# A fused sliding-window attention and gated feed-forward kernel: an attention burst one gap later, another batch's bursts re-placed, and two more transposes given to the DMA crossbar

## The chip, the cores and the metric

The kernel runs on one core of a Trainium2 chip. The metric is the device time of one execution in microseconds; the time of a kernel is the median of several executions. Beside these times there is one execution recorded by the hardware profiler, with its trace. All positions below are microseconds from the start of that recording.

## The reference

Eight batches of eight heads attend over 576 positions with head size 64. A query sees the keys within 32 positions, eight global positions see everything, and everything sees them. The attention output is the input of a gated feed-forward block over 4608 tokens.

```python
    scores = scale * np.matmul(q, k.transpose(0, 1, 3, 2))
    mask = np.abs(pos[:, None] - pos[None, :]) <= window
    mask = mask | is_global[:, None] | is_global[None, :]
    scores = np.where(mask, scores, -1000000000.0)
...
    attn = np.exp(scores)
    attn = attn / (np.sum(attn, axis=-1, keepdims=True) + 1e-09)
    return np.matmul(attn, v).astype(np.float32)
...
    x = np.ascontiguousarray(attn_out.transpose(0, 2, 1, 3)).reshape(B * S, H * D)
    g = x @ w_gate
    silu = g * (1.0 / (1.0 + np.exp(-g)))
    val = x @ w_val
    return (silu * val @ w_out).astype(np.float32)
```

## The kernel before

The feed-forward block is the backbone. Its 4608 tokens are cut into nine chunks of 512, and each chunk is 16 *units* on TensorE: twelve `gate` units (lines 782 to 798), each eight matmuls of 512 columns into two banks of PSUM, and four `outp` units (lines 845 to 857) of twelve such matmuls each. After every unit comes a *gap*, into which the program puts small pieces of attention work. Gaps are numbered through, 16 to a chunk; the loop at lines 926 to 933 emits unit n and then the pieces of gap n. The order on each engine is the order in which the program emits: nothing is reordered later, so an instruction that waits holds up everything behind it on its engine.

Attention of batch b is spread over the gaps of the chunk before the one that needs it. `attention(b)` (line 348) returns a table from a relative gap number to a list of steps. The table of batch 1 is shifted by 3 (line 908) and that of batch b from 2 on by 16(b-1) (line 910). So relative gap 7 of batch 1 is gap 10, and relative gap 2 of batch 2 is gap 18. The steps of one batch:

- `step_GT` (line 399) transposes the gathered global keys and queries on TensorE; VectorE copies them out as `gT`.
- `step_S2` (line 438): scores of all keys against the global columns. It reads `kT`. ScalarE takes the exponential (`p2e`), VectorE masks it into `p2` (line 454).
- `step_SG` (line 416): scores of the global rows. It reads `qTs[b]`, that is `qT`. Result: `pg`.
- `step_P2T` (line 460): transposes `p2` into `p2t`. Below batch `XP` it does so by five transposes on TensorE and a copy on ScalarE; from batch `XP` on by one crossbar transpose, a DMA that SyncE issues (line 463).
- `step_AV2` (line 473): value products of the global rows from `p2t` and `va`; VectorE makes `gv` of them (lines 484 to 492).
- `step_S(u)`, u from 0 to 4 (line 497): local scores, 16 small matmuls (8 for u = 4), an exponential on ScalarE and a multiplication by the band on VectorE.
- `step_AV(tp)`, tp from 0 to 3, and `step_AV8` (lines 574 and 606): value products of 128 tokens each from the local probabilities, `pg` and `gv`. They read `va` and `vb`, a copy of `va` shifted by 64 rows. VectorE then normalises (lines 562 to 568). The PSUM pool "m" has one buffer, which most value products share, so a product waits until the one before it is normalised.
- `step_X` (line 630), `step_X01`, `step_X8`: transposition of the result into `xT`, the input of the gate units. From batch 2 on this is a crossbar transpose issued by SyncE.

From batch 2 on k and q arrive in three stages. GpSimd issues DMAs that cast k and q to bf16 in DRAM (`cast_qk`, line 106); SyncE issues crossbar transposes from there into `kT` and `qT` (`transpose_qk`, line 114, the issues at lines 116 and 120); TensorE reads these. `load_v` (line 97) has GpSimd load `va` in five blocks, and `load_vb` (line 124) has SyncE copy `va` to `vb` in two DMAs (lines 129 and 130).

SyncE's instructions are one queue in program order: `kT` and `qT` of batch b, results `out` (line 857), `vb`, `p2t` where it is a DMA, and the transposes of `xT`. For batch 2 the queue around the change reads: `kT`, `qT` of batch 2; four results; two `vb` of batch 2; `kT`, `qT` of batch 3; then the transposes of the results of batch 2.

Of the kernel before, what the change touches and what calls it, by code (L numbers as in the profile page):

```python
# [26 lines left out]
def kernel(  # L27
# [25 lines left out]
    KC = S + 2 * WIN  # L53
    XQ = 2
    XB = 2
    XP = 4
    W = D + 2

    assert (B, H, S, D, NG, DM, DF) == (8, 8, 576, 64, 8, 512, 1536)
# [288 lines left out]
    def attention(b):  # L348
# [111 lines left out]
        def step_P2T():  # L460
            if b >= XP:
                st["p2t"] = work.tile([P, 5, P], BF16, tag="p2t", name="p2t")
                nc.sync.dma_start_transpose(out=st["p2t"], in_=st["p2"])
                return
            ps = mtile([P, 5, P], BF16, "ps_p2t")
            for u in range(5):
                nc.tensor.transpose(
                    out=ps[:, u, :], in_=st["p2"][:, P * u : P * (u + 1)], identity=ident
                )
            st["p2t"] = work.tile([P, 5, P], BF16, tag="p2t", name="p2t")  # L470
            nc.scalar.copy(out=st["p2t"], in_=ps)
# [231 lines left out]
        L = lambda f, *a: (lambda: f(*a))  # L703
# [30 lines left out]
        if b == 1:  # L734
            return r | {
                5: [L(step_P2T), L(step_S, 0)],
                6: [L(step_S, 1), L(step_AV2)],
                7: [L(step_S, 2), L(step_AV, 0)],
                8: [L(step_S, 3), L(step_AV, 1)],
                9: [L(step_AV, 2)],  # L740
                10: [L(step_AV, 3), L(step_X01, 0)],
                11: [L(step_S, 4), L(step_X01, 1)],
                12: [L(step_AV8)], 13: [L(step_X8)],
            }
# [10 lines left out]
        if b == 2:  # L755
            return {
                1: [L(step_GT), vb],
                3: [L(step_S2), L(step_SG)],
                4: [L(step_S, 0), L(step_P2T)],
                6: [L(step_S, 1), L(step_AV2)],  # L760
                8: [L(step_S, 2), L(step_AV, 0), L(step_X, 0)],
                10: [L(step_S, 3), L(step_AV, 1), L(step_X, 1)],
                11: [L(step_S, 4), L(step_AV, 2), L(step_X, 2)],
                12: [L(step_AV, 3), L(step_AV8), L(step_X, 3), L(step_X8)],
            }
        return {
            1: [L(step_GT), vb],
            2: [L(step_S2), L(step_SG)] + ([L(step_P2T)] if b >= XP else []),
            4: [L(step_S, 0)] + ([] if b >= XP else [L(step_P2T)]),
            7: [L(step_S, 1), L(step_AV2)],  # L770
# [90 lines left out]


    head, xa1, xa2, xa3, s4, av8, x8 = attention(0)
    for f in head:
        f()
# [41 lines left out]
    for i, g in attention(1).items():  # L907
        gaps[3 + i] = gaps.get(3 + i, []) + g
    for b in range(XQ, B):
        o = 16 * (b - 1)  # L910
        for i, g in attention(b).items():
            gaps[o + i] = gaps.get(o + i, []) + g
        if b > 3:
            tr_at[b] = o - 16 + 5
        if b > 4:
            cast_at[b] = o - 32 + 8
        if b > 2:
            v_at[b] = o - 16 + 2
            if b % 2 == 0:
                g_at[b] = o - 16 + 6  # L920
                m_at[b] = o - 16 + 13
# [43 lines left out]
```

## Time and profile before

| | us |
|---|---|
| median of 5 runs | 358.0 (357.56 to 358.96) |
| the profiled execution | 357.52 |
| its span in the trace | 355.7 |
| TensorE busy | 344.5 (97%) |
| VectorE busy | 232.1 (65%) |
| ScalarE busy | 151.8 (43%) |
| GpSimd busy | 92.6 (26%) |

The granted TensorE clock is 1.00 over the whole span. The profiled execution is 0.48 us below the median of the runs, and 1.8 us of it lie outside the span. By stage, from the view of busy time in given stretches (busy time of TensorE and VectorE, mean busy share of the core's DMA engines):

| stretch, us | what runs there | TensorE | VectorE | DMA |
|---|---|---|---|---|
| 40.0 to 66.5 | rest of chunk 0, batch 1's attention | 25.82 of 26.50 | 15.14 | saturated, 182 GB/s |
| 66.5 to 93.0 | gates of chunk 1, batch 2's attention | 25.85 of 26.50 | 22.44 | saturated, 181 GB/s |
| 104.6 to 142.0 | chunk 2, batch 3's attention | 37.03 of 37.40 | 25.72 | saturated, 173 GB/s |
| 142.0 to 179.0 | chunk 3, batch 4's attention | 36.74 of 37.00 | 25.52 | 144 GB/s |

A gate unit takes TensorE about 1.73 us, an output unit about 2.6 us. A DMA in the trace has the time of its issue on its engine's queue, and a landing time, which is when its completion reached the semaphore that a reader waits for.

### The profile page before, as it was taken

What the parts mean: (1) busy time and instruction counts of PE and PEld (TensorE: products, weight loads), DVE (VectorE), ACT (ScalarE), POOL (GpSimd) and SP (SyncE); (2) the same over time, 40 slices, a digit from 0 to 9 for tenths busy, and PEclk for the clock granted to TensorE, in tenths of its full rate; (3) what the DMA queues carried; (4) which work ended last, traced back from release to release, by engine and by line L of the source; (5) the groups of instructions that cost most, each with busy time, mean ns of one, the idle gap of its engine ahead of it and who ended that gap; (6) DMA issues with size and microseconds to landing.
All of it is one profiled execution on the core that took longest, in us unless ns stands there. A gap on an engine that the chain in (4) does not pass through costs nothing.

```text
span 355.7 us, 7680 instructions
## 1 busy us (share of the span) xinstructions
PE 344.5 (97%) x3112; PEld 167.8 (47%) x3161; DVE 232.1 (65%) x470; ACT 151.8 (43%) x235; POOL 92.6 (26%) x110
## 2 busy tenths in 40 slices
PE   6989999999999999999999999999999999999996
PEld 2575545444444454444444444444444444444444
DVE  5868784389818873789368935894488637815850
ACT  4865662465325541554244523543254323323322
POOL 8984663905323314301290111000000000000000
PEclk9999999999999999999999999999999999999999
DMA  7999999999999999995899979813320230011002
GB/s 108 150 197 204 184 212 160 146 251 142 158 172 233 145 156 163 173 183 82 147 166 152 141 120 168 113 42 92 105 70 2 61 100 28 0 59 62 0 20 100
DMA packets 153540, 44.15 MB, mean 124 GB/s; under 512 B 140064, under 2 KB 148000, under 8 KB 153504
## 3 DMA queue, kind: packets, MB, share of 16 engines
q0 software_dynamic: 101216, 19.14, 68.3%
q1 hardware_dynamic: 52288, 24.51, 34.0%
q8 instruction: 25, 0.41, 0.5%
q14 instruction: 11, 0.09, 0.1%
HBM read 38.02 MB, written 16.52 MB: 153 GB/s over the span
## 4 chain that ended last, share of the span: by engine, by line
PE 84%; DMA 9%; POOL 4%; issue 1%; DVE 1%; ACT 0%; POOLq 0%
PE po L850 25%; PE pg L793 24%; PE pv L793 23%; DMA va<-in_v_dram 4%; DMA k_bf<-in_k_dram 3%; PE ps_av L595 3%; PE ps_s L508 3%; DMA vb<-va 2%; PE ps_av L586 1%; PE po L837 1%; POOL va L102 1%; PE ps_av L477 1%; PE ps_s L442 1%; PE ps_av L622 0%; PE ps_av L614 0%
## 5 line engine op out<-in xcount | busy, mean ns | idle before, releaser
L793 PE MATMUL pg<-xT,wg_sb 128*128 128x512 bf16 x399 | 107.0, 380 | 1.6
L793 PE MATMUL pv<-xT,wv_sb 128*128 128x512 bf16 x413 | 106.6, 379 | 0.1
L822 DVE SCALAR_TENSOR_TENSOR gv<-th,pg 128x512 bf16<-128x512 bf16 x107 | 73.3, 685 | 50.2 <-ACT th L820 49.3
L820 ACT ACTIVATE th<-pg 128x512 bf16<-128x512 f32 x107 | 63.9, 598 | 81.4 <-PE pg L793 79.5
L850 PE MATMUL po<-wo_sb,h 128*128 128x512 bf16 x400 | 92.4, 379 | 0.9 <-issue 0.2
L826 DVE TENSOR_TENSOR h<-gv,pv 128x512 bf16<-128x512 bf16 x107 | 73.5, 687 | 11.5 <-PE pg L793 0.5
L793 PEld LDWEIGHTS <-wv_sb 128*128 128x128 bf16 x424 | 41.5, 98 | 50.0
L850 PEld LDWEIGHTS <-h 128*128 128x128 bf16 x420 | 39.5, 98 | 45.4
L793 PEld LDWEIGHTS <-wg_sb 128*128 128x128 bf16 x424 | 38.4, 98 | 43.5 <-issue 1.7
L102 POOL DMA_DIRECT2D va<-in_v_dram x40 | 35.5, 993 | 82.7 <-PE ps_av L595 72.4
L855 ACT ACTIVATE osb<-po 128x512 f32<-128x512 f32 x35 | 20.9, 597 | 81.9 <-PE po L850 60.8
L541 ACT ACTIVATE pe<-ps_s 128x1024 bf16<-128x1024 f32 (+1 forms) x39 | 36.4, 936 | 17.0 <-PE ps_s L508 17.0
L547 DVE TENSOR_TENSOR pt<-pe,band 128x1024 bf16<-128x1024 bf16 (+1 forms) x39 | 24.7, 634 | 14.0 <-ACT pe L541 13.9
L568 DVE TENSOR_TENSOR xa<-ps_av,den 128x512 bf16<-128x512 f32 (+1 forms) x40 | 25.5, 638 | 1.4
L562 DVE TENSOR_REDUCE den<-ps_av 128x8 f32<-128x16 f32 (+1 forms) x40 | 6.7, 166 | 27.6 <-PE ps_av L595 25.2
L508 PEld LDWEIGHTS <-kT 64*128 64x128 bf16 x576 | 10.7, 95 | 15.5 <-issue 15.1
L109 POOL DMA_DIRECT2D kf<-in_k_dram x6 | 13.4, 2233 | 16.5 <-issue 10.2
L109 POOL DMA_DIRECT2D qf<-in_q_dram x6 | 15.4, 2564 | 3.9 <-DMA va<-in_v_dram 2.4
L508 PE MATMUL ps_s<-qT,kT 64*128 64x64 bf16 x576 | 15.3, 191 | 0.1
L595 PE MATMUL ps_av<-vb,pt 128*64 128x66 bf16 x256 | 14.2, 197 | 0.5 <-DMA vb<-va 0.5
L595 PE MATMUL ps_av<-va,pt 128*64 128x66 bf16 x256 | 14.4, 197 | 0.0
L595 PEld LDWEIGHTS <-pt 128*64 128x64 bf16 x512 | 10.8, 110 | 4.7 <-DMA vb<-va 0.6
(142 smaller groups left out, 198.3 us busy)
## 6 DMA issues: line engine op xcount, KB each, us to landing
out_dram<-osb SPq DMA_DIRECT2D x35, 256.0 KB, 2.6
vb<-va SPq DMA_DIRECT2D x14, 264.0 KB, 5.3
kf<-in_k_dram POOLq DMA_DIRECT2D x6, 576.0 KB, 18.3
qf<-in_q_dram POOLq DMA_DIRECT2D x6, 576.0 KB, 18.4
va<-in_v_dram POOLq DMA_DIRECT2D x24, 128.0 KB, 10.8
va<-in_v_dram POOLq DMA_DIRECT2D x16, 96.0 KB, 9.1
wg_sb<-in_moe_w_gate_dram POOLq DMA_DIRECT2D x3, 512.0 KB, 11.7
wv_sb<-in_moe_w_val_dram POOLq DMA_DIRECT2D x3, 512.0 KB
```

The costliest lines, as they stand in the source:

```text
L102: nc.gpsimd.dma_start(out=va[lo:hi, u, :, 0:D], in_=vs[t0 + lo : t0 + hi])
L109: nc.gpsimd.dma_start(out=t, in_=src[b].rearrange("h s d -> s h d"))
L508: nc.tensor.matmul(out=ps[:, par, 64 * slot : 64 * slot + 64], lhsT=kT[r : r + 64, hp, 64 * t : 64 * t + P], rhs=qTs[b][r : r + 64, hp, 64 ...
L541: nc.scalar.activation(out=pe, in_=ps[:, :, 0 : 64 * ns].rearrange("p r (s c) -> p r s c", c=64), func=AF.Exp, scale=SCALE,)
L547: mult = lambda: nc.vector.tensor_tensor(out=pt.rearrange("p r s c -> p (r s) c"), in0=pe.rearrange("p r s c -> p (r s) c"), in1=bc(band, ...
L568: nc.vector.tensor_tensor(out=xa.rearrange("p (g h) d -> p g h d", g=g), in0=bc(ps, pst + [[1, D]]), in1=bc(den, [[4, g], [1, 4], [0, D]]) ...
L595: nc.tensor.matmul(out=ps[64 * e : 64 * e + 64, hg, hl, :], lhsT=pt[:, hl % 2, 4 * (hl // 2) + 2 * (tp % 2) + e, :], rhs=(va if e == 0 els ...
L793: nc.tensor.matmul(out=ps[:, 0:n], lhsT=w[:, cc, P * fc : P * (fc + 1)], rhs=xT[:, cc, t0 : t0 + n], start=(cc == 0), stop=(cc == NCC - 1),)
L820: nc.scalar.activation(out=th[:, 0:n], in_=pg[:, 0:n], func=AF.Tanh, scale=0.5)
L822: nc.vector.scalar_tensor_tensor(out=gv[:, 0:n], in0=th[:, 0:n], scalar=1.0, in1=pg[:, 0:n], op0=ALU.add, op1=ALU.mult,)
L826: nc.vector.tensor_tensor(out=st["h"][:, fc, 0:n], in0=gv[:, 0:n], in1=pv[:, 0:n], op=ALU.mult)
L850: nc.tensor.matmul(out=po, lhsT=st["h"][:, fc, P * ts : P * (ts + 1)], rhs=wo_sb[:, fc, :], start=(fc == 0), stop=(fc == NFC - 1),)
```

## The change

Three edits:

1. `XP` goes from 4 to 2. `step_P2T` of batches 2 and 3 becomes the crossbar transpose that batches 4 to 7 already use (line 463). In the table of batches 3 and up (line 766) this also moves the step of batch 3 from relative gap 4 to relative gap 2.
2. In batch 1 the value products `step_AV` 0, 1 and 2 come one gap later: from relative gaps 7, 8, 9 to 8, 9, 9.
3. In batch 2 `step_S2`, `step_SG` and `step_P2T` go to relative gap 2 (from 3, 3 and 4). `step_S` 2 with `step_AV` 0, and `step_S` 3 with `step_AV` 1, come one gap earlier (7 and 9 in place of 8 and 10).

```diff
-    XP = 4
+    XP = 2
...
             return r | {
                 5: [L(step_P2T), L(step_S, 0)],
                 6: [L(step_S, 1), L(step_AV2)],
-                7: [L(step_S, 2), L(step_AV, 0)],
-                8: [L(step_S, 3), L(step_AV, 1)],
-                9: [L(step_AV, 2)],
+                7: [L(step_S, 2)],
+                8: [L(step_S, 3), L(step_AV, 0)],
+                9: [L(step_AV, 1), L(step_AV, 2)],
                 10: [L(step_AV, 3), L(step_X01, 0)],
...
         if b == 2:
             return {
                 1: [L(step_GT), vb],
-                3: [L(step_S2), L(step_SG)],
-                4: [L(step_S, 0), L(step_P2T)],
+                2: [L(step_S2), L(step_SG), L(step_P2T)],
+                4: [L(step_S, 0)],
                 6: [L(step_S, 1), L(step_AV2)],
-                8: [L(step_S, 2), L(step_AV, 0), L(step_X, 0)],
-                10: [L(step_S, 3), L(step_AV, 1), L(step_X, 1)],
+                7: [L(step_S, 2), L(step_AV, 0), L(step_X, 0)],
+                9: [L(step_S, 3), L(step_AV, 1), L(step_X, 1)],
                 11: [L(step_S, 4), L(step_AV, 2), L(step_X, 2)],
                 12: [L(step_AV, 3), L(step_AV8), L(step_X, 3), L(step_X8)],
```

On the engines: TensorE has ten transposes and ScalarE two copies less. SyncE's queue has two DMAs more, each directly behind the two `vb` copies of its batch and ahead of `kT` and `qT` of the next batch. VectorE and GpSimd have the same instructions, VectorE in another order.

## The prediction, made before the changed kernel ran

> **What bounds the kernel now.** I read the page first, for the engine that sets the end:
>
> ```profile
> PE 344.5 (97%) x3112; PEld 167.8 (47%) x3161; DVE 232.1 (65%) x470; ACT 151.8 (43%) x235; POOL 92.6 (26%) x110
> PE 84%; DMA 9%; POOL 4%; issue 1%; DVE 1%; ACT 0%; POOLq 0%
> ```
>
> TensorE (PE) is busy 97% of the span and 84% of the chain that ended last; the DMA share lies before 50 us. So a microsecond put into or taken from TensorE's order is a microsecond of time, and a wait on TensorE counts in full. Next I asked what TensorE waits for, from 20 us on: only four waits remain.
>
> ```profile
> PE ps_av L595 <- DMA vb<-va: 0.5, 1, 0.5
> PE ps_av L586 <- DVE xa L568: 0.4, 1, 0.4
> PE ps_x L646 <- DVE xa L568: 0.2, 1, 0.2
> PE po L850 <- issue: 0.2, 1, 0.2
> ```
>
> The first is batch 1's first value product, the second batch 2's third one. Then the timeline of TensorE (start, length, instruction) around batch 2's global scores, where the change moves most:
>
> ```profile
> 71.96 1.03 PE L793 MATMUL pg<-xT,wg_sb 128*128 128x512 bf16 x4
> 72.82 1.03 PE L793 MATMUL pv<-xT,wv_sb 128*128 128x512 bf16 x4
> 73.78 0.46 PE L442 MATMUL ps_s<-kT,gT 128*32 128x320 bf16 x8
> 74.06 0.42 PE L420 MATMUL ps_sg<-qT,gT 128*32 128x288 bf16 x8
> 74.41 1.04 PE L793 MATMUL pg<-xT,wg_sb 128*128 128x512 bf16 x3
> ...
> 76.59 0.45 PE L467 MATMUL ps_p2t<-ident,p 128*128 128x128 bf16 x5
> 76.88 1.03 PE L793 MATMUL pg<-xT,wg_sb 128*128 128x512 bf16 x4
> ...
> 80.76 0.47 PE L477 MATMUL ps_av<-va,p2t 128*32 128x132 bf16 x20
> ```
>
> L442 is `step_S2`, L420 `step_SG`, L467 `step_P2T`, L477 `step_AV2`. Last, the queue of SyncE at the same place, and the time from issue to landing of its `qT` and of its second `vb`, each asked for alone:
>
> ```profile
> 63.06 5.22 SPq L120 DMA_TRANSPOSE qT<-qf  x1
> 68.32 2.05 SPq L857 DMA_DIRECT2D out_dram<-osb  x4
> 70.60 0.47 SPq L129 DMA_DIRECT2D vb<-va  x1
> 71.16 0.55 SPq L130 DMA_DIRECT2D vb<-va  x1
> ```
> ```profile
> DMA to landing us min/median/max: 10.9/10.9/10.9
> ```
> ```profile
> DMA to landing us min/median/max: 9.3/9.3/9.3
> ```
>
> The reader should add: `qT` of batch 2 lands at 63.06 + 10.9 = 73.97, and `step_SG`, which waits for it in the program, starts at 74.06. It has no slack to come earlier. `vb` lands at 71.16 + 9.3 = 80.5.
>
> **What the Trainium skill says.** "DMA: Bandwidth & Descriptors", section "Queues, rings and completion order": SyncE's DMAs share one row of rings, each engine takes descriptors in ring order, and takes turns with other rows packet by packet. So `p2t` starts behind what SyncE issued before and shares with GpSimd's casts. The trace agrees: batch 7's `p2t`, in an idle system, lands 2.6 us after issue, batch 5's 7.6 us, under load. "TensorE: Matmul & The Clock Gate", section "What's actually happening": an idle window of about 3.4 us halves TensorE's clock. No run here shows it; from 20 us on TensorE never idles 1 us, and the clock stays at 1.00.
>
> **The change part by part.** The sum is made against the profiled execution, 357.52 us, of which 355.7 is span; it is 0.48 below the median, and I carry the difference over to the median.
>
> Batch 1. Its first product stops between 49.14 and 49.83 for `vb`, which landed at 49.78; two such matmuls otherwise start 0.05 apart, so 0.64 is lost. One gap later means one gate unit (1.73) and `step_S` later, about 51.0, and the wait is gone: -0.64 locally. What is late next: product 1 shares the one "m" buffer and needs product 0 normalised. Exponential (1.02), band (0.69) and normalisation (0.17 + 0.20 + 0.69 with gaps between) end near 54.1; TensorE, with an output unit of 2.6 between, comes at 54.3. It fits by 0.2; a miss would cost tenths, and they would vanish in the next wait.
>
> Batch 2, `step_SG`. `step_S2` in gap 18 stands where the next gate unit started, 71.96, less the 0.64: about 71.3. Its inputs are there (`kT` landed 56.81 + 11.6 = 68.4; `gT` was copied by 71.8, less the shift 71.1). It takes 0.28. `step_SG` then waits from 71.6 to the landing of `qT`. That landing is not moved by TensorE: the transposes wait for the cast of k, and the casts, loads and issues ahead of them are those of before. So TensorE idles about 2.4 us, starts `step_SG` at about 74.02, and still has before it the gate unit that ran from 71.96 to 73.78, now 1.73 back to back. Against before: 74.02 - 74.06 + 1.73 = +1.69. The gain of batch 1 is inside this sum: it only lengthens the wait.
>
> Batch 2, transpose. Five transposes leave TensorE: 76.88 - 76.59 = -0.29; ScalarE's copy (0.69) was hidden, worth nothing. `step_AV2` would then start at 80.76 + 1.69 - 0.29 = 82.16. `p2` is ready about 73.3 (S2 at 71.3, 0.5 to ScalarE, 0.70 there, VectorE's `h` until 72.8, then 0.48); SyncE is free, since the next item, `kT` of batch 3, waited for its cast until 80.67 anyway. Issue at 73.3, so 8.9 us are available. But four results of 256 KB and two `vb` of 264 KB stand ahead, and `vb` lands only at 80.5. Lower bound: `p2t` follows with the last `vb` packets and lands 81.7 to 82.2: cost 0. Upper bound: `vb`'s landing plus the 3.3 us by which batch 4's `p2t` followed its `vb` (157.1, read from the semaphores, against 153.8): 83.8; with a late ring 84.5, cost 2.3. I take 83.0, as GpSimd's casts keep the DMA engines full until 85: +0.8. Behind this waiting instruction stands all of TensorE.
>
> Batch 2, products. With gaps 7, 9, 11 in place of 8, 10, 11 the third product no longer finds the "m" buffer occupied: -0.39 (the wait of 0.4 above). Product 0 now comes one unit after `step_AV2`; before, `gv` was finished 2.8 us after the start of `step_S` 1 (80.42 to 83.25), and the product would ask 2.7 us after it: 0 to +0.1, and nothing if `step_AV2` is late, as VectorE then is ahead. I take 0.
>
> Batch 3. Five transposes leave: -0.29. `p2` is ready at 111.73 before and `step_AV2` starts 120.42 - 0.29 = 120.13, so 8.4 us for the landing; batch 4 had 8.4 (149.13 to 157.51) and no wait. I take 0; at most some tenths. On SyncE the new item waits for `p2`, so `kT` and `qT` of batch 4, issued at 107.17 and 114.14, move some 6 to 7 us back. They are read from 147 on, and the next item, the first `xT` of batch 3, came at 127.66 after 6 us of idle queue. That idle time hides it. The `xT` transposes of batch 2 stay where the landing of k and q of batch 3 puts them; the third landed 0.3 us before chunk 2's first gate at 104.60, which now comes over 1 us later.
>
> Sum: +1.69 - 0.29 + 0.8 - 0.39 - 0.29 = +1.5. So 357.52 + 1.5 = 359.0 for a profiled execution and 358.0 + 1.5 = 359.5 as a median. A measurement of this kernel can tell about 0.3%, 1.07 us, from no change.
>
> **The rivals.**
>
> The wait for `qT` stands, but `p2t` is hidden: +0.7, 358.7. For it: 8.9 us from issue exceed the 7.6 and 8.0 of batches 5 and 4. Against it: these had less queued ahead and casts did not run so full.
>
> Faster: `qT` of batch 2 lands in time. One mechanism, its place is line 420 in gap 18. Its landing follows a cast of 13 us under full DMA, which can differ between executions. At a landing of 73.25 the sum without a late `p2t` is zero; at 71.6 or before, nothing waits and all gains stand: -0.64 - 0.29 - 0.39 - 0.29 = -1.6, 356.4. Against it: the profile has it at 73.97, and its last completion lags its data because GpSimd's queue was full from 70 to 73.
>
> Clock: the idle stretch of 2.4 us, with `p2t`'s soon after, makes TensorE slow. Estimated from the page's 3.4 us window at half speed: 1.7 more, 361.2. Against it: 2.4 is below the window.
>
> That the change doesn't do what it says is excluded for the orders; for edit 2 the waits eat what it brings.
>
> **How the numbers follow.** Forecast (wait for `qT`, `p2t` 0.1 to 2 late) 0.65, with +0.8 to +2.7; `p2t` hidden 0.17; `qT` in time 0.12; clock or a `p2t` still later 0.06. Slower by over 0.3%: about 0.9 of the first, the last, and little else: 0.65. Faster: 0.12. Within 0.3%: 0.23. The range leaves out the faster case and the top of the slow one: 357.9 to 361.0.
>
> **What would show it.** In the changed profile: a TensorE wait of about 2.4 us at L420 near 72 to 74, ended by the DMA of `qT`; none at L595 near 49; a wait of about 0.8 at L477 near 82, ended by the DMA of `p2t`, landing 9 to 10 us after issue; none at L586 near 92; batch 3's L477 without a wait. The prediction is wrong if L420 doesn't wait, or if `p2t` of batch 2 lands after 85.

## The result and the profile after

The changed kernel takes 359.09 us (median of 42 executions, 357.39 to 363.38), the kernel before 358.08 (79 executions). The ratio is 1.0025 with a 95% interval of 1.0012 to 1.0037: slower by 0.9 us, or by 1.0 if the two medians are subtracted. Here and below the ratio is the one on record; it is not the quotient of the medians, but every interval covers that quotient too. The profiled execution took 358.02 us, 0.5 more than that of before; its span is 356.3.

TensorE's waits of the changed kernel from 20 us on, all of them (who waited, for whom: us in total, times, longest):

```profile
PE ps_sg L420 <- DMA qT<-qf: 1.3, 1, 1.3
PE ps_x L646 <- DVE xa L568: 0.2, 1, 0.2
PE po L850 <- issue: 0.2, 1, 0.2
PE pg L793 <- issue: 0.2, 1, 0.2
```

The two waits that the change was to remove (L595 for `vb`, L586 for the normalised product) are gone, and one has come that before did not have. The timeline of TensorE, changed kernel:

```profile
70.42 1.03 PE L793 MATMUL pv<-xT,wv_sb 128*128 128x512 bf16 x4
71.37 0.46 PE L442 MATMUL ps_s<-kT,gT 128*32 128x320 bf16 x8
73.12 0.43 PE L420 MATMUL ps_sg<-qT,gT 128*32 128x288 bf16 x8 [1.30 <-DMA qT<-qf]
...
81.28 0.47 PE L477 MATMUL ps_av<-va,p2t 128*32 128x132 bf16 x20
...
93.08 2.76 PE L850 MATMUL po<-wo_sb,h 128*128 128x512 bf16 x12
```

`step_SG` stands idle until `qT` lands (SyncE's issue at 62.01, 11.1 to landing, so 73.1). `step_AV2` starts at 81.28, when `p2t` has just come (81.15): issued at 73.15, with this time to landing:

```profile
DMA to landing us min/median/max: 8.0/8.0/8.0
```

The view of the weight loads' waits has one more, at chunk 2's first gate:

```profile
PEld L793 <- DMA xT<-xa: 0.6, 1, 0.6
```

TensorE would have reached this gate at 104.63, as before. It is the landing that moved: the third transpose of batch 2's `xT` landed at about 104.9, in the profile of before at 104.3.

Starts of the same instructions in the two profiles give the ledger. It is TensorE's alone; the rest of the span's 0.6 lies behind the start of the last output unit.

| landmark | before | changed | difference | step since the line above |
|---|---|---|---|---|
| first gate after the head (44) | 44.15 | 44.17 | +0.02 | |
| batch 2 `step_GT` | 70.12 | 69.44 | -0.68 | -0.70 batch 1 |
| batch 2 `step_AV2` | 80.76 | 81.28 | +0.52 | +1.20 `qT`, less `step_P2T` |
| first output unit of chunk 1 | 93.05 | 93.08 | +0.03 | -0.49 spread of the products |
| first gate of chunk 2 | 104.60 | 104.89 | +0.29 | +0.26 wait for `xT` |
| batch 3 `step_AV2` | 120.42 | 120.45 | +0.03 | -0.26 `step_P2T` off TensorE |
| last output unit | 349.90 | 349.98 | +0.08 | +0.05 |

So every gain arrived, and in this execution two waits took them back almost exactly. The timed executions lose more, 0.9 us. The mean granted clock of 44 executions of the changed kernel (these 42 and two more) is on record: it is 0.998 or more in 32, median 358.6; 0.994 or 0.995 in 10, median 360.9; and 0.990 in two, 363.3 and 363.4. The executions at a lower clock are followed below.

### The profile page after: what moved, and what is told of

It is laid out like the page before. It is cut to its first block, busy times and chain, and to the rows that moved or that the text cites. A ratio compares the mean times of both kernels' runs of the same rounds, so it can differ in the third digit from the quotient of the medians.

```text
span 356.3 us, 7661 instructions
## 1 busy us (share of the span) xinstructions
PE 344.5 (97%) x3102; PEld 167.3 (47%) x3151; DVE 231.8 (65%) x470; ACT 150.7 (42%) x233; POOL 92.5 (26%) x110
## 4 chain that ended last, share of the span: by engine, by line
PE 90%; DMA 5%; DVE 1%; issue 1%; ACT 1%; POOL 0%; POOLq 0%
PE pg L793 26%; PE po L850 25%; PE pv L793 24%; PE ps_s L508 3%; PE ps_av L595 3%; DMA qT<-qf 3%; DMA q_bf<-in_q_dram 2%; PE ps_av L586 1%; PE ps_av L477 1%; PE po L837 1%; PE ps_t L385 1%; PE ps_t L365 1%; PE ps_sg L420 1%; PE ps_s L442 1%; PE pg L809 1%
## 5 line engine op out<-in xcount | busy, mean ns | idle before, releaser
L109 POOL DMA_DIRECT2D kf<-in_k_dram x6 | 13.4, 2238 | 19.4 <-issue 11.1
L595 PE MATMUL ps_av<-va,pt 128*64 128x66 bf16 x256 | 14.2, 197 | 0.0
L595 PE MATMUL ps_av<-vb,pt 128*64 128x66 bf16 x256 | 14.2, 197 | 0.0
L595 PEld LDWEIGHTS <-pt 128*64 128x64 bf16 x512 | 10.7, 110 | 4.1
## 6 DMA issues: line engine op xcount, KB each, us to landing
wg_sb<-in_moe_w_gate_dram POOLq DMA_DIRECT2D x3, 512.0 KB, 10.5
```

What stands on the lines that cost most here:

```text
L109: nc.gpsimd.dma_start(out=t, in_=src[b].rearrange("h s d -> s h d"))
L595: nc.tensor.matmul(out=ps[64 * e : 64 * e + 64, hg, hl, :], lhsT=pt[:, hl % 2, 4 * (hl // 2) + 2 * (tp % 2) + e, :], rhs=(va if e == 0 els ...
```

## The experiments

Theory "landings": `qT`, `p2t` and `xT` of batch 2 arrive when the DMAs bring them, wherever TensorE stands, and hold it in turn. Rivals: "late p2t" alone, and "clock", the fourth case of the prediction.

**Edit 1 alone** (`step_AV` of batch 1 later; the rest as before)

> Only batch 1's value products are moved (edit 1); all else is the kernel before. The wait at L595 for vb near 49 is gone and TensorE runs 0.6 to 0.8 us ahead up to 104. If the landing of batch 2's third xT transpose (104.3 in the profile of before, 105.0 in that of the changed kernel) is what chunk 2's first gate waits for, TensorE waits there, L793 on the DMA of xT, 0.3 to 0.9 us, and the time is 357.6 to 358.1 (gain 0 to 0.4). If nothing waits there, the full 0.7 is kept: 357.4.

357.76 against 358.26, ratio 0.9991 (0.9972 to 1.0009): a small gain in the median, not clear of noise. In the profile no wait at L595 is left. TensorE is 0.4 behind before at 44, after a wait of 0.4 for `q_bf` at 32, then 0.3 ahead at `step_GT` of batch 2, and 0.2 ahead at the end. So edit 1 brought its 0.7 here, and 0.6 of it lasted. The wait for `xT` that was expected did not come; TensorE was hardly ahead at that gate.

**SG one gap later**

```diff
-                2: [L(step_S2), L(step_SG), L(step_P2T)],
+                2: [L(step_S2), L(step_P2T)],
+                3: [L(step_SG)],
```

> The changed kernel with step_SG of batch 2 back in relative gap 3, step_S2 and the crossbar transpose staying in gap 2. Theory qT (the extra time is the wait at L420): that wait is gone. TensorE then comes to L477 at about 80.0, but p2t, issued at 73.2 as before, lands at 81.2: a wait of about 1.2 moves to L477, and the time stays within 0.3 us of the changed kernel. Theory late p2t (in the timed executions p2t lands after 82 and that is the extra time): the same time too, with a longer wait at L477, 2 us or more. Theory clock (the idle stretch at L420 costs granted clock in a quarter of the executions): executions at 0.995 become rare, and the median falls by 0.4 or more.

359.29 against 358.26, ratio 1.0016 (0.9998 to 1.0034). Waits of TensorE in this kernel:

```profile
PE ps_av L477 <- DMA p2t<-p: 2.4, 1, 2.4
PE ps_x L646 <- DVE xa L568: 0.2, 1, 0.2
PE pg L794 <- DMA xT<-xa: 0.2, 1, 0.2
```

L420 waits no more, and the wait stands at L477, as expected of both landing theories: with `qT` out of the way, `p2t` (9.3 us from issue here) is next. At 2.4 us it is of the size that "late p2t" gave, not the 1.2 of the other. Of the clock theory one half came: a single execution of 22 is at 0.995; the median did not fall.

**Transpose of batch 2 on TensorE, SG still in gap 2**

```diff
-    XP = 2
+    XP = 3
...
-                2: [L(step_S2), L(step_SG), L(step_P2T)],
-                4: [L(step_S, 0)],
+                2: [L(step_S2), L(step_SG)],
+                4: [L(step_S, 0), L(step_P2T)],
```

> The changed kernel with batch 2's step_P2T on TensorE again, in gap 4 (XP = 3); step_S2 and step_SG stay in gap 2. Theory qT: the wait at L420 stays, 1.3 to 2.4 us, TensorE has 0.29 more work: 0 to 0.4 us slower than the changed kernel. Theory late p2t: the wait at L477 in the timed executions is gone, 0.5 us or more faster than the changed kernel. Theory clock: as many executions at 0.995 as with the change.

359.53 against 358.26, ratio 1.0038 (1.0019 to 1.0058). The wait for `qT` remains, and 0.5 for the normalised product:

```profile
PE ps_sg L420 <- DMA qT<-qf: 2.2, 1, 2.2
PE ps_av L586 <- DVE xa L568: 0.5, 1, 0.5
```

Without a DMA for batch 2's `p2t` the loss is not smaller. "Late p2t" as the main cause falls. Seven of 22 executions are at 0.995 or lower, about as many as with the change, as the clock theory had it.

**S2 and SG in gap 3, transpose of batch 2 on TensorE in gap 4** (`XP = 3`)

> The changed kernel with batch 2's step_S2 and step_SG back in gap 3 and its step_P2T on TensorE in gap 4 (XP = 3); edit 1, the even spread of the products and batch 3's crossbar transpose stay. Theory qT: neither L420 nor L477 waits, TensorE is 1.0 to 1.3 us ahead of before at 93 and reaches chunk 2's first gate at about 103.5, where it waits for xT until 104.3 to 105; with batch 3's 0.29 the time is 0.2 to 0.6 us below before (357.5 to 357.9). If the landing of xT does not bind: 1.3 below before, 356.8. Theory late p2t: the same. Theory clock: executions at 0.995 as rare as before the change.

358.83 against 358.26, ratio 1.0005 (0.9985 to 1.0024): not clear of the kernel before, and not clear of the changed kernel either. The expected gain is missing, and L420 waits, which theory "qT" excluded. The profile shows what TensorE, ahead after batch 1, still meets: `qT` (landing 74.2 here) and `xT`. One execution of 22 is at 0.995.

```profile
PE pg L793 <- DMA xT<-xa: 1.1, 1, 1.1
PE ps_sg L420 <- DMA qT<-qf: 0.7, 1, 0.7
```

**Relieved of all three**: S2, SG and the transpose on TensorE in gaps 3, 4 and 5; SyncE's order changed:

```diff
+        if b != 3:
+            transpose_q(b)
...
+    at(27, transpose_q, 3)
```

> A version meant to take TensorE off all three landings. Against the changed kernel: batch 2's step_S2 in gap 3, its step_SG in gap 4, its step_P2T on TensorE in gap 5; SyncE issues qT of batch 3 only after the third xT transpose of batch 2, and batch 3's step_SG moves to relative gap 3. Theory of three landings (qT at 73 to 74.5, p2t at 81 to 82.5, xT at 104.3 to 106 hold TensorE in turn): no DMA wait at L420 or L477 or at chunk 2's first gate, TensorE about 1.0 us ahead of before at 93 and at 105, with batch 3's 0.29 the end 1.1 to 1.4 us before: 356.7 to 357.1. If instead some other work holds chunk 2 (a DMA wait at batch 3's SG because qT now lands after 111): 357.5 or more. Rival (the loss lies in the granted clock or elsewhere, not in landings): the time stays at 358 or above.

357.92 against 357.96, ratio 1.0001 (0.9988 to 1.0013). The view of busy time in given stretches (us; TensorE, weight loads, VectorE, ScalarE, GpSimd busy; clock; DMA share; GB/s) shows TensorE without a gap where the landings stood, and one longer wait before them:

```profile
66.50:93.00 26.50, 26.50 (x271) 12.60 (x269) 22.41 (x42) 14.06 (x21) 10.07 (x10) 1.00 1.84 180
93.00:120.00 27.00, 26.98 (x208) 12.13 (x206) 15.34 (x32) 9.80 (x16) 10.80 (x11) 1.00 1.78 182
```
```profile
PE ps_av L599 <- DMA vb<-va: 0.9, 1, 0.9
```

(L599 is before's L595.) In the profile the three waits are gone, and chunk 2 begins 0.8 earlier than before. The time does not follow: the changed kernel's loss is gone, but the expected 357.1 or less is missed by about 1 us, and 357.92 is almost the value of the rival. Since the waits and the lower clock go together here (none of the 14 executions is below 0.998), this run cannot tell the two apart. Which wait takes the 0.8 in the median execution, one profile cannot say; the `vb` of batch 1, too late here even for its new gap, is a candidate. That is open.

**The wait filled**: seven unused matmuls between S2 and SG of the changed kernel

> The changed kernel with seven unused matmuls of 512 columns (1.5 us, the kernel's own warm helper, results not read) between batch 2's step_S2 and step_SG, so that TensorE isn't idle while it waits for qT. Theory landings: the 1.5 us lie inside the wait of 1.3 to 2.4 us, the time of the middle execution changes by 0 to +0.3 us. Theory clock (the idle stretch costs granted clock in a quarter of the executions): executions above 360 fall from 12 of 42 to about the share of before, 9 of 75, and the mean falls by 0.3 to 0.5 us. Without that theory the share stays near a quarter.

359.70 against 357.96, ratio 1.0048 (1.0031 to 1.0065), 3 of 11 executions above 360. As they were put, neither expectation holds: it is slower than the change, and the share above 360 is no smaller (of before, 6 of 75 are above 360, not 9). But those three executions have a clock of 0.999 or 1.000. The lower clock itself shows in 1 of 11, the profiled one, and there it fell to half in the head, at 18 to 22 us, behind a 1.55 us wait for `va` in batch 0, and not behind L420. So the count of the clock leans to the clock theory; 11 executions do not settle it. In the profile the filling ended just with the landing (64.40 + 10.5 = 74.9, SG at 74.94), so it did no harm there; TensorE was 1.4 us behind the changed kernel's profile from the head on, and batch 3's `p2t` cost 0.3. Why this kernel is slow at full clock too is open.

**Batch 3's transpose alone** (`XP = 3` in the kernel before), and **the spread of batch 2's products alone**

> The kernel before with batch 3's transpose alone given to the crossbar (XP = 3, batch 2's tables as before). Five transposes leave TensorE, 0.29 us, p2t lands 8.1 us after issue as in the changed kernel, just before L477: no wait. Time 0.2 to 0.3 us below before. Rival (kT and qT of batch 4, issued 6 us later, or the xT transposes of batch 3 come too late): a DMA wait at L420 near 147 or at L793 near 142, and no gain or a loss.

> The kernel before with batch 2's step_S 2 and 3 and step_AV 0 and 1 one gap earlier, nothing else. The wait of 0.4 at L586 for the normalised product is gone, TensorE is 0.4 to 0.5 us ahead at 93. Theory landings: it then waits at chunk 2's first gate, L793 for xT, whose landing is set by SyncE's queue and not by TensorE, 0.1 to 1 us: the time is that of before within 0.3 us. Rival (xT comes earlier along with the products): the gain of 0.4 is kept, 357.7 to 357.8.

358.70 and 357.79 against 357.96; ratios 1.0008 (0.9989 to 1.0027) and 0.9998 (0.9985 to 1.0012). Both local gains appear on TensorE: 0.28 from chunk 2's first gate to batch 3's `step_AV2` in the first, 0.49 from batch 2's `step_AV2` to chunk 1's first output unit in the second. Neither shows in the time. The first waits 0.7 us for `vb` of batch 1 and 1.1 for batch 2's `xT`, both ahead of its edit, in an execution 1.2 above its median. The second was 1.1 behind before already at 44 and found `vb` late by 0.8; the expected wait for `xT` did not come. There is no late `qT` near 147 and no wait near 142 in the first: that rival falls.

**The change again, and with 1.08 us of work before and behind the landings**

```diff
-                12: [L(step_AV8)], 13: [L(step_X8)],
+                12: [L(step_AV8), L(warm, *[512] * 5)], 13: [L(step_X8)],
```

(this one before; the one behind has the same `warm` in batch 3's gap 4)

> The changed kernel once more, unaltered, as the measure for the three others on the same chip. 0.2 to 0.4% above before (358.6 to 359.5 where before has 358.0); in its profile a wait of 1 to 2.5 us at L420 on the DMA of qT.

> The changed kernel with five unused matmuls of 512 columns (1.08 us of TensorE, results not read) in gap 15, ahead of batch 2's wait at L420. Theory landings (qT arrives when the DMAs bring it, wherever TensorE stands): the work vanishes in the wait, which shrinks from 1.3 to 2.5 us by 1.1; the time is that of the changed kernel, +0.2 at most. Rival (the wait moves with TensorE, or the loss lies elsewhere): +0.8 to +1.1 us over the changed kernel.

> The same five unused matmuls in gap 36, behind all three landings (qT, p2t and xT of batch 2). Both theories: nothing hides them, the time is 1.0 to 1.2 us above the changed kernel. If it is less, some later wait has slack that the traces do not show.

On this chip before has 357.87. Unaltered, the changed kernel has 360.09, ratio 1.0074 (1.0041 to 1.0107), more than was expected; with the work before 360.56, 1.0060 (1.0042 to 1.0079); with it behind 361.08, 1.0096 (1.0064 to 1.0129). By the ratios the work before costs nothing and the work behind 0.8 us; by the medians they cost 0.5 and 1.0. With 6 to 8 executions each the intervals overlap, and the times do not decide between the landing theory and its rival.

The traces say this much. With the work behind, TensorE's lag on the changed kernel's first profile grows from 0.58 to 1.66, the full 1.08. Against the repeat on this chip it grows only from 0.30 to 1.03, because the repeat itself waits 0.3 us for batch 3's `p2t` there: a fourth landing, which the theory did not name. With the work before, the wait at L420 did not shrink: it is 2.4 us, for `qT` landed at 75.1, in the repeat at 73.2. The inserted work stands at 65.8, behind SyncE's issue of `qT` at 63.62 (62.39 in the repeat), so it did not delay that issue. That the wait swallows such work is not shown by this pair.

The profile of the kernel with work before gave what the filled wait did not. Its timeline:

```profile
72.36 0.46 PE L442 MATMUL ps_s<-kT,gT 128*32 128x320 bf16 x8
75.19 0.43 PE L420 MATMUL ps_sg<-qT,gT 128*32 128x288 bf16 x8 [2.37 <-DMA qT<-qf]
75.55 1.83 PE L793 MATMUL pg<-xT,wg_sb 128*128 128x512 bf16 x4
77.17 1.91 PE L793 MATMUL pv<-xT,wv_sb 128*128 128x512 bf16 x4
78.88 1.12 PE L793 MATMUL pg<-xT,wg_sb 128*128 128x512 bf16 x4
```

and busy time in stretches, same columns as above:

```profile
75.00:76.00 1.00, 0.81 (x10) 0.34 (x11) 0.00 (x0) 0.33 (x1) 0.00 (x0) 0.83 1.26 333
76.00:79.00 3.00, 3.00 (x9) 1.08 (x8) 1.14 (x2) 0.92 (x2) 0.00 (x0) 0.50 1.20 316
79.00:82.00 3.00, 3.00 (x29) 1.32 (x28) 1.91 (x3) 1.35 (x2) 0.00 (x0) 0.99 1.80 147
```

Directly behind the wait for `qT` the granted clock is 0.50. The gate unit there takes 3.33 us (75.55 to 78.88) in place of 1.73: 1.6 us lost on top of the wait. The mean clock of that execution is 0.994, a value of the slower ones above. The last run below has the same: a wait of 1.97 us at SG, then half clock. A count over all runs agrees:

| kernels | executions | of these at 0.995 or lower |
|---|---|---|
| before, on three chips | 136 | 12 |
| batch 2's SG in relative gap 2 behind an empty wait (the change, the transpose on TensorE, work before, work behind, `xT` earlier) | 92 | 34 |
| the same, with the wait filled | 11 | 1 |
| the others, SG in gap 3 or 4 | 116 | 5 |

The contrast holds on single chips too: 7 of 22 with SG in gap 2 against 4 of 66 with SG in gap 3 on one, 15 of 26 against none of 13 of before on another. So the clock theory is shown for this place, as a part of the loss that comes in about a third of the executions.

**The landing of xT made earlier** (SyncE's order of "relieved" in the changed kernel)

> The changed kernel with SyncE issuing batch 3's qT only after the third xT transpose of batch 2, and batch 3's step_SG in relative gap 3. Theory landings: the wait at chunk 2's first gate (0.3 us in the changed kernel's profile, more where TensorE is early) goes, those at L420 and L477 stay: 0.2 to 0.6 us below the changed kernel, at or above before. Rival (xT was no bound): the changed kernel's time within 0.2 us.

361.74, ratio 1.0100 (1.0074 to 1.0126), on the same chip as the 1.0074: no gain, a miss. There is no wait for `xT` in the profile, but the execution waited 0.6 us for `vb` of batch 1 and 2.0 at SG, and had a half-clock stretch behind SG as well. With these in front, TensorE reached chunk 2 at 107.25, too late for `xT` to matter, so whether `xT` is a bound stays open. Behind it came a wait of 0.7 for batch 3's `p2t`. Five of 6 executions are at 0.995 or lower, 4 of 8 with the change unaltered.

## Why the prediction was right

Slower was forecast as likeliest, by 1.5 us; 0.9 was measured, inside the range. At 0.25% it is smaller than the 0.3% that the prediction called clearly slower. The place and the kind of the main loss were right. The size owes something to luck: the sum had two terms too large, and two that the runs show were not in it.

- Bound: TensorE's order and its waits set the time, as read. Busy time is the same 344.5 us in both profiles.
- Batch 1, -0.64: -0.70 in the profile; the next product came without waiting. That the wait for `qT` swallows this gain fits the ledger: with the measured start of `step_SG` the prediction's sum gives 73.12 - 74.06 + 1.73 = +0.79, less 0.29 for the transposes +0.50, and the ledger has +0.52 at `step_AV2`. No experiment shows it apart from that.
- `step_SG`: a wait of 2.4 from 71.6 to 73.97 was forecast; it was 1.3 in this profile, because `qT` landed at 73.1, and 1.5 to 2.4 in the five later profiles with SG in gap 2 and nothing in the wait. The mechanism and the place hold. The size follows a landing that differs by up to 2 us between executions, mostly because SyncE's issue of `qT` does (61.7 to 64.4 over fourteen profiles, then 10.5 to 11.9 us to the landing). The prediction took one profile's landing as fixed.
- `p2t` of batch 2, +0.8 from 83.0: it landed at 81.2, below the lower bound of 81.7, as the `vb` ahead of it landed at 79.7 and not at 80.5. It followed that `vb` by 1.4 us, and by 1.2 to 2.1 in the seven profiles that have this DMA; the forecast leaned too far to the 3.3 of batch 4. With SG in gap 2 the term was zero in all six such profiles. Only with SG one gap later did TensorE meet it, for 2.4 us.
- Products of batch 2: -0.49 for -0.39. Batch 3: -0.26 for -0.29, `p2t` 8.1 us from issue with 8.4 available, no wait. In three other profiles it took 8.7 to 9.3 us and TensorE waited 0.3, 0.3 and 0.7: the "some tenths" of the prediction.
- `xT` at chunk 2: the step "which now comes over 1 us later" was wrong for this profile, where TensorE came at 104.63, and so was the landing that "stays". It moved from 104.3 to 104.9 and cost 0.26.
- The clock was a rival with 0.06 for itself. It is no case beside the forecast but part of it: behind the wait for `qT`, in some executions, at 1.6 us each. Its argument against, that 2.4 us lie below the window, failed. At full clock (0.998 or more) the changed kernel has 358.62, and before 358.18, 357.92 and 357.87 on three chips: 0.4 to 0.8 of loss, about the rival with `p2t` hidden (+0.7). The rest, 0.3 to 0.6, goes with the lower clock, which 12 of 44 executions show, and 12 of 136 of before. The split is rough, as the chips differ.

## What to carry to other kernels

Before moving a consumer earlier, look up when its input lands, not only whether it waited: an instruction that starts 0.1 us behind a landing shows no wait and has no slack. Several such landings in a row can take back the gains ahead of them, so a local saving must be followed to the next one. A landing differs between executions, here by up to 2 us, so one profile gives its place only roughly. A stall of two microseconds on TensorE can cost nearly as much again in clock: 1.6 us behind the wait of 2.37.

## What the runs showed of the hardware that was not expected

The Trainium skill, "TensorE: Matmul & The Clock Gate", section "What's actually happening", gives an idle window of about 3.4 us for the fall to half clock. Here a wait of 1.97 us and one of 2.37 were followed by it, and one of 1.55 in the head of another, while waits of 1.8 and 2.2 at L420 and of 2.4 at L477 in other executions were not: the measurements decide, and a stall well below the window is not safe. In all three cases the half clock then lasted 3.4 us. The same section says that the window runs freely, so how a stall lies against it could explain the difference; that was not tested.

The landing of one crossbar transpose, `p2t` of batch 2, took 8.0 and 9.3 us in two executions of nearly equal orders, and `qT` landed between 73.1 and 75.1 in the thirteen profiles that show its landing.
